# A retention layer and a bilinear FFN on one core: the output product of the last three tiles by Strassen's seven products

## The chip, the cores and the metric

The kernel runs on one core of a Trainium2 chip. The metric is the device time of one execution in microseconds (us). The kernel before took 224.37 us, the median of three runs (224.01 to 226.11).

The engines that appear below: TensorE (PE, with its weight loads as PEld) does the matmuls into PSUM, VectorE (DVE), ScalarE (ACT) and GpSimd (POOL) do everything elementwise, and SyncE (SP) issues the DMAs.

## The reference

Inputs are q, k and v of shape (4, 8, 768, 64), that is batch, heads, sequence and head size, and three weight matrices. For each batch and head a state of 64 x 64 decays by a factor gamma per step, and the tokens' results go through a bilinear FFN:

```python
for t in range(S):
    state = gamma[None, :, None, None] * state + np.einsum('bhd,bhe->bhde', k[:, :, t], v[:, :, t])
    y[:, :, t] = scale * np.einsum('bhd,bhde->bhe', q[:, :, t], state)
x = attn_out.transpose(0, 2, 1, 3).reshape(B * S, H * D)      # 3072 x 512
a = x @ w_a                                                   # 512 x 1536
b = x @ w_b                                                   # 512 x 1536
out = a * b @ w_out                                           # 1536 x 512, float32
```

## The kernel before, in words

The 3072 tokens are 24 **slots** of 128. `TILES = [4, 2, 2, 2, 2, 4, 4, 4]` groups the slots into eight FFN tiles J, of 512 or 256 tokens. The FFN's hidden size of 1536 is twelve chunks ft of 128.

**The FFN.** One *block* (J, ft) is `ffn_ab`: four matmuls `a` (L536, over the four chunks kt of the model size), a ScalarE copy of `a` to `asb` (L540), four matmuls `g` (L548), and a VectorE product `ht = g * asb` (L551), in bf16. After twelve blocks come the *outputs* (J, "o", i): for each slot i, `ffn_out` runs twelve matmuls of 512 columns with `ht` as the stationary operand and `wo_bf` as the moving one (L576), ScalarE copies the bank to `osb` (L180, called from L578), and SyncE stores it (L563 or L586). All of it is bf16 with float32 sums in PSUM. The banks `a`, `g`, `o` and one of the state banks come from one pool of three, `psff`.

**The retention.** Tokens are worked two slots at a time. `casts(t)` on GpSimd scales k and q of a slot by tables of the decay, to `kqb` (L210), and casts v (L182). A DMA transpose makes `kqT` (L223), and after the second slot of a pair the loads of the next pair are issued on SyncE (`load_slot`, L89), in the same queue as the transposes and the stores. A *turn*, `turn(new, old)`, is the TensorE work for two slots. It first runs the casts and leaves that are left in the list `later` (`catch_up`). For the older slots it does the first half of `inter` (q times the state, L320), for the newer ones `chunk_states` (k times v, L255, summed by VectorE into `sums`, L269, and cast to `gst`) and `scores` (k times q, L279, masked by VectorE into `aT`, L285), and for the older ones the second half of `inter` and `intra` (v times the masked scores, L332). Between the halves the rows of a PSUM bank change hands, so a *fence* is kept: a copy of one column, `mark`, on ScalarE or VectorE (L297), waits for the last matmul ahead of it, and the second half of `inter` waits for that copy. At the end `leave` copies the result to the FFN's input `xt` (L343, L349, L350).

**What sets the order.** Each engine runs its instructions in the order in which the code issues them (`seq`). The table `ahead` (L689 to L701) names what is issued ahead of each block or output: `(5, "o", 0): [(turn, 18, 16)]` is a turn ahead of tile 5's first output. Casts and leaves in `later` are issued by `catch_up`, two after each block, all of them ahead of an output.

## Time and profile before

| | |
|---|---|
| Time, median of three runs | 224.37 us (224.01 to 226.11) |
| Span of the profiled execution | 222.2 us (it has no time of its own beside the span) |
| Granted TensorE clock | full speed in all slices of the span |
| TensorE busy | 214.4 us |
| VectorE, ScalarE, GpSimd busy | 96.8, 93.7, 79.5 us |
| Matmuls of the outputs, L576 | 62.5 us busy in 299 matmuls |
| Matmuls `a` and `g`, L536 and L548 | 77.2 and 77.5 us busy, 401 each |
| GpSimd waiting for k (DMA) | 31.5 us |

Busy time of TensorE counts overlapping matmuls once. A row of a group reads: line, engine, operation, output and inputs, partitions by elements and type, count; then busy time in all and mean nanoseconds of one; then the idle time of that engine just ahead of them and what ended it. A row of the timeline reads: start, duration, engine, line, operation, count.

### The profile page before, as it was taken

The page shows a single profiled execution, that of the slowest core. Times are in us where ns is not written, and L with a number is a line of the kernel's source. Part 1 is how long each engine was busy: PE and PEld are TensorE (multiplying, and loading weights), DVE is VectorE, ACT ScalarE, POOL GpSimd, SP SyncE. Part 2 cuts the span into 40 slices and gives each one's busy share as a digit, 9 for nine tenths or more (in the row PEclk, how much of TensorE's full clock was granted, in tenths as well). Part 3 has the DMA queues.
Part 4 walks back from the last instruction along what each step waited for, and adds up shares of the span by engine and source line. Part 5 has one row for each costly group of instructions (what it writes and reads, how often), then busy time and mean ns, then how long its engine had stood idle before and what let it go on. Part 6 is the DMA issues. An engine that isn't in the chain of part 4 may idle for free.

```text
span 222.2 us, 6261 instructions
## 1 busy us (share of the span) xinstructions
PE 214.4 (96%) x2613; PEld 131.3 (59%) x2633; DVE 96.8 (44%) x199; ACT 93.7 (42%) x201; POOL 79.5 (36%) x105
## 2 busy tenths in 40 slices
PE   7799999999999999999999999999999999999994
PEld 6578655785457867867865444554444544444443
DVE  2783437641525535472475344533333621334300
ACT  3775244441535435443456333455333444333221
POOL 5557799682544335351613535350000000000000
PEclk9999999999999999999999999999999999999999
DMA  6999999999999988999969898984100012100022
GB/s 180 347 378 382 366 312 398 299 210 200 228 236 266 242 197 129 227 211 204 219 145 228 115 248 220 216 181 131 47 0 0 3 50 94 47 3 0 3 94 94
DMA packets 96124, 39.72 MB, mean 179 GB/s; under 512 B 76000, under 2 KB 91616, under 8 KB 96096
## 3 DMA queue, kind: packets, MB, share of 16 engines
q1 hardware_dynamic: 95952, 39.20, 68.5%
q8 instruction: 20, 0.33, 0.6%
q10 hardware_dynamic: 144, 0.13, 0.2%
q14 instruction: 8, 0.07, 0.1%
HBM read 28.31 MB, written 6.29 MB: 156 GB/s over the span
## 4 chain that ended last, share of the span: by engine, by line
PE 92%; DMA 3%; POOL 1%; issue 1%; DVE 1%; SPq 0%; ACT 0%; ACTq 0%; POOLq 0%
PE g L548 28%; PE a L536 28%; PE o L576 28%; DMA kf<-in_k_dram 3%; PE y L320 1%; POOL kqb L210 1%; PE at L279 1%; PE y L332 1%; PE st L255 1%; PE tp L395 1%; PE st L436 1%; DVE aT L420 1%; SPq L95 0%; PE at L408 0%; PE y L459 0%
## 5 line engine op out<-in xcount | busy, mean ns | idle before, releaser
L551 DVE TENSOR_TENSOR ht<-g,asb 128x256 bf16<-128x256 f32 (+1 forms) x98 | 53.9, 550 | 82.6 <-PE g L548 73.4
L548 PE MATMUL g<-xt,wb_bf 128*128 128x256 bf16 (+1 forms) x401 | 77.5, 317 | 0.2
L536 PE MATMUL a<-xt,wa_bf 128*128 128x256 bf16 (+1 forms) x401 | 77.2, 317 | 0.1
L540 ACT CAST asb<-a 128x256 bf16<-128x256 f32 (+1 forms) x98 | 46.3, 472 | 71.3 <-PE a L536 69.3
L576 PE MATMUL o<-wo_bf,ht 128*128 128x512 bf16 (+2 forms) x299 | 62.5, 362 | 1.4 <-issue 1.1
L536 PEld LDWEIGHTS <-wa_bf 128*128 128x128 bf16 x404 | 39.2, 98 | 23.5 <-DVE xt L182 0.4
L548 PEld LDWEIGHTS <-wb_bf 128*128 128x128 bf16 x404 | 39.4, 98 | 22.5
L576 PEld LDWEIGHTS <-ht 128*128 128x128 bf16 x312 | 28.8, 98 | 30.6
L210 POOL TENSOR_TENSOR kqb<-kf,ktab 128x512 bf16<-128x512 f32 x21 | 22.3, 1065 | 39.9 <-DMA kf<-in_k_dram 31.5
L180 ACT COPY osb<-o 128x512 f32<-128x512 f32 (+2 forms) x25 | 14.1, 564 | 36.1 <-PE o L576 27.8
L182 POOL CAST vb<-vf 128x512 bf16<-128x512 f32 x24 | 14.4, 610 | 23.0 <-DMA vf<-in_v_dram 18.5
L210 POOL TENSOR_TENSOR kqb<-qf,qtab 128x512 bf16<-128x512 f32 x21 | 22.3, 1063 | 0.1
L269 DVE TENSOR_TENSOR sums<-st,sums 128x256 f32<-128x256 f32 x30 | 12.7, 424 | 1.6
L180 ACT CAST gst<-sums 128x256 bf16<-128x256 f32 x26 | 10.4, 406 | 5.1 <-DVE sums L269 2.4
L285 DVE TENSOR_TENSOR aT<-at,mask 128x512 bf16<-128x512 f32 x18 | 11.5, 681 | 0.0
L343 ACT CAST xt<-y 128x512 bf16<-128x512 f32 x16 | 8.5, 584 | 0.7 <-PE y L332 0.7
L182 POOL CAST wo_bf<-wsto 128x1024 bf16<-128x1024 f32 x6 | 6.2, 1040 | 2.5 <-DMA wsto<-in_moe_w_out_dram 2.5
L182 POOL CAST wa_bf<-wsta 128x1024 bf16<-128x1024 f32 (+1 forms) x7 | 6.4, 919 | 1.7 <-DMA wsta<-in_moe_w_a_dram 1.6
L182 POOL CAST wb_bf<-wstb 128x1024 bf16<-128x1024 f32 (+1 forms) x7 | 6.4, 918 | 1.5 <-DMA wstb<-in_moe_w_b_dram 1.3
L395 PE MATMUL tp<-ident,kqb 128*128 128x128 bf16 x48 | 4.5, 220 | 1.6 <-DVE kqb L210 0.9
L320 PEld LDWEIGHTS <-gst 64*64 64x64 bf16 x264 | 3.7, 106 | 3.4 <-issue 3.4
L297 DVE COPY lgr<-bq 128x1 f32<-128x1 f32 x4 | 0.6, 154 | 11.2 <-PE y L320 11.2
(63 smaller groups left out, 99.2 us busy)
## 6 DMA issues: line engine op xcount, KB each, us to landing
out_dram<-osb SPq DMA_DIRECT2D x23, 256.0 KB, 2.7
kf<-in_k_dram SPq DMA_DIRECT2D x18, 256.0 KB, 4.2
qf<-in_q_dram SPq DMA_DIRECT2D x18, 256.0 KB, 4.4
vf<-in_v_dram SPq DMA_DIRECT2D x18, 256.0 KB, 4.9
wsta<-in_moe_w_a_dram SPq DMA_DIRECT2D x6, 512.0 KB, 7.6
wstb<-in_moe_w_b_dram SPq DMA_DIRECT2D x6, 512.0 KB, 7.8
wsto<-in_moe_w_out_dram SPq DMA_DIRECT2D x6, 512.0 KB, 8.5
kf<-in_k_dram SPq DMA_DIRECT2D x3, 512.0 KB, 5.9
```

What stands on the lines that cost most here:

```text
L180: seq(nc.scalar.copy(dst, src))
L182: seq(engine.tensor_copy(dst, src))
L210: seq(eng.tensor_tensor(dst, src, tab, op=ALU.mult))
L269: seq(nc.vector.tensor_tensor(new, u[c][:, s], old, op=ALU.add))
L285: seq(nc.vector.tensor_tensor(aT[n][:, r].rearrange("p s h d -> p (s h) d"), at[:, r].rearrange("p s h d -> p (s h) d"), mask.to_broadcast ...
L343: seq(nc.scalar.copy(dst, ys[o][c]))
L395: seq(nc.tensor.transpose(tp[:, m, hp, :], kqb[2 * u + par][:, i, hp, :, :], ident))
L536: seq(nc.tensor.matmul(a[:, b0 - c0 : b1 - c0], wa_bf[:, kt, fs], xcols(J, kt, b0, b1), start=(kt == 0 and b0 == c0), stop=(kt == KT - 1 a ...
L540: seq(nc.scalar.copy(asb, a))
L548: seq(nc.tensor.matmul(g[:, b0 - c0 : b1 - c0], wb_bf[:, kt, fs], xcols(J, kt, b0, b1), start=(kt == 0 and b0 == c0), stop=(kt == KT - 1 a ...
L551: seq(nc.vector.tensor_tensor(ht[J][:, ft, c0:c1], g, asbs.pop((J, ft, c0)), op=ALU.mult))
L576: seq(nc.tensor.matmul(o, ht[J][:, ft, i * P : (i + 1) * P], wo_bf[:, ft, c0:c1], start=(ft == 0), stop=(ft == NFT - 1)))
```

## The change

**The output product.** For tiles J >= `FAST` = 5, `ffn_out` per slot gives way to `ffn_fast` per pair of slots. The h of two slots (rows of even and odd tokens), the two chunks of a hidden pair (r = 0, 1) and the two halves of the 512 output columns form 2 x 2 blocks, and Strassen's algorithm in Winograd's form makes the four output blocks with seven products in place of eight. Each product is six matmuls of 256 columns. Four of the seven take sums of h (`hsum`, four per tile), which VectorE forms in bf16 block by block (`add`, by the table `adds`). Four take sums and differences of the weights (`wt_bf`): four VectorE operations and a ScalarE copy for each of six chunks, `combine_o`, after the outputs of tile 0 and the first of tile 1. Two banks are added to several times, R1 four times and R5 twice; between the additions ScalarE copies the bank to `snap`, or VectorE adds it to a copy.

**Layout.** In all tiles the columns of a pair of slots now stand even tokens first. To that end q of the later slots is loaded in two DMAs of 64 partitions instead of one of 128, the mask of the scores and the tables for q follow the new order (with another table on GpSimd), `queries` picks the columns of `kqT`, and a pair of slots is stored with one DMA of 512 KB instead of two of 256 KB. The late tables' VectorE and ScalarE part moves from the start into block 6 of tile 0.

**Order.** The turn (18, 16) moves from tile 5's first output to its block 8, the turn (22, 20) from tile 6's first output to its block 6, and the turn (None, 22) from tile 6's third output to its first. The marks of turns are always on ScalarE (before, four were on VectorE), casts to `gst` too, and leaves always come ahead of those casts. The masking of scores is put off by a block or output (`mask_now`). In the last leaves (turn without new slots) VectorE does both halves.

```diff
+FAST = 5
...
+            if nm == "q":
+                s = s.rearrange("h (n par) d -> par n h d", par=2)
+                for par in range(2):
+                    seq(nc.sync.dma_start(out=raws[nm, t][64 * par : 64 * par + 64], in_=s[par]))
+            else:
+                seq(nc.sync.dma_start(out=raws[nm, t], in_=s.rearrange("h p d -> p h d")))
...
+    def combine_o(j):
+        st = wst["o", j].rearrange("p r (c d) -> p r c d", c=2)
+        b11, b12, b21, b22 = st[:, 0, 0], st[:, 0, 1], st[:, 1, 0], st[:, 1, 1]
+        tmp = tra.tile([P, 2, DH], F32, tag="aT", name="tmp")
+        seq(nc.vector.tensor_tensor(tmp[:, 0], b12, b11, op=ALU.subtract))
+        seq(nc.vector.tensor_tensor(tmp[:, 1], b22, tmp[:, 0], op=ALU.subtract))
+        seq(nc.vector.tensor_tensor(wt_bf[:, j, 2], b22, b12, op=ALU.subtract))
+        seq(nc.vector.tensor_tensor(wt_bf[:, j, 3], b21, tmp[:, 1], op=ALU.subtract))
+        seq(nc.scalar.copy(wt_bf[:, j, :2], tmp))
...
             for s in range(2):
-                seq(nc.vector.tensor_tensor(dst[:, s, on], ys[o][c][:, s, on], part[:, s], op=ALU.add))
-                seq(nc.scalar.copy(dst[:, s, off], ys[o][c][:, s, off]))
+                seq(nc.vector.tensor_tensor(dst[:, s, on], src[:, s, on], part[:, s], op=ALU.add))
+                seq(nc.vector.tensor_copy(dst[:, s, off], src[:, s, off]))
...
             if new is not None:
-                fence[old, 0] = fence[old, 1] = fenced(eng)
+                fence[old, 0] = fence[old, 1] = fenced(nc.scalar)
...
+    def add(J, which, f0, f1):
...
+        x, y, op = {
+            0: (lambda: rows(J, 0, 1, f0, f1), lambda: rows(J, 1, 1, f0, f1), ALU.add),
+            1: (lambda: s[0], lambda: rows(J, 0, 0, f0, f1), ALU.subtract),
+            2: (lambda: rows(J, 0, 0, f0, f1), lambda: rows(J, 0, 1, f0, f1), ALU.subtract),
+            3: (lambda: rows(J, 1, 0, f0, f1), lambda: s[1], ALU.subtract),
+        }[which]
+        seq(nc.vector.tensor_tensor(s[which], x(), y(), op=op))
+
+    def product(R, J, u, left, right, first):
+        for f in range(NH):
+            if left[0] == "h":
+                r, par = left[1:]
+                lhs = ht[J][:, 2 * f + r, (2 * u + par) * P : (2 * u + par + 1) * P]
+            else:
+                lhs = hsum[J][left[1]][:, f, u]
+            w, m = right
+            seq(nc.tensor.matmul(R[:, :DH], lhs, (wo_bf, wt_bf)[w][:, f, m, :],
+                                 start=(first and f == 0), stop=(f == NH - 1), skip_group_check=True))
+
+    def ffn_fast(J, u):
+        osb, dst = placed[J, u] = place(J, u)
...
+        R1 = bank()
+        product(R1, J, u, ("h", 0, 0), (0, 0), True)
+        seq(nc.scalar.copy(snap[:, 0], R1[:, :DH]))
+        catch_up(2)
+        R6 = bank()
+        product(R6, J, u, ("h", 1, 0), (0, 2), True)
+        seq(nc.vector.tensor_tensor(osb[:, 0, :DH], R6[:, :DH], snap[:, 0], op=ALU.add))
+        mask_now(1)
+        catch_up(1)
+        store()
+        product(R1, J, u, ("s", 1), (1, 1), False)
+        seq(nc.scalar.copy(snap[:, 1], R1[:, :DH]))
+        catch_up(1)
+        R5 = bank()
+        product(R5, J, u, ("s", 0), (1, 0), True)
+        seq(nc.scalar.copy(snap[:, 2], R5[:, :DH]))
+        catch_up(1)
+        product(R1, J, u, ("s", 2), (1, 2), False)
+        seq(nc.vector.tensor_tensor(osb[:, 1, DH:], R1[:, :DH], snap[:, 2], op=ALU.add))
+        mask_now(1)
...
+        product(R5, J, u, ("s", 3), (0, 3), False)
+        seq(nc.vector.tensor_tensor(osb[:, 0, DH:], R5[:, :DH], snap[:, 1], op=ALU.add))
+        mask_now()
+        if ends:
+            seq(nc.sync.dma_start(out=dst[:, 0], in_=osb[:, 0]))
+        catch_up(1)
+        product(R1, J, u, ("h", 1, 1), (1, 3), False)
+        seq(nc.scalar.copy(osb[:, 1, :DH], R1[:, :DH]))
...
-        (1, "o", 1): [(turn, 8, 6, D_, True), (casts, 10)],
+        (1, "o", 1): [(turn, 8, 6), (casts, 10)],
...
-        (5, 2): [(casts, 21)], (5, "o", 0): [(turn, 18, 16)], (5, "o", 1): [(casts, 22)],
-        (5, "o", 2): [(turn, 20, 18, D_)], (5, "o", 3): [(casts, 23)],
-        (6, "o", 0): [(turn, 22, 20)], (6, "o", 2): [(turn, None, 22)],
+        (5, 2): [(casts, 21)], (5, 8): [(turn, 18, 16), (casts, 22)],
+        (5, "o", 2): [(turn, 20, 18), (casts, 23)],
+        (6, 6): [(turn, 22, 20)], (6, "o", 0): [(turn, None, 22)],
     }
...
+    adds = {3: [(0, 0, 2)], 4: [(1, 0, 2)], 5: [(2, 0, 2)], 6: [(3, 0, 2)],
+            7: [(0, 2, 4)], 8: [(1, 2, 4)], 9: [(2, 2, 4)], 10: [(3, 2, 4), (0, 4, 5)],
+            11: [(1, 4, 5), (0, 5, 6), (1, 5, 6), (2, 4, 5), (2, 5, 6), (3, 4, 5), (3, 5, 6)]}
...
+    combined = {(0, 0): (0, 1), (0, 1): (2,), (0, 2): (3,), (0, 3): (4,), (1, 0): (5,)}
```

What stands in a row on an engine, at three places. The first is ScalarE around the turn (8, 6), between tile 1's two outputs, before (the numbers of `gst` are those of its eight buffers):

```order
L180 COPY osb<-o 128x512 x3
L343 CAST xt<-y 128x2x4x64 x2
L180 CAST gst_157<-sums 128x256
L180 CAST gst_158<-sums 128x256
L180 COPY osb<-o 128x512
```

and after:

```order
L634 COPY osb<-o 128x512
L221 CAST wt_bf<-tmp 128x512
L337 COPY mark<-bq 128x1
L387 CAST xt<-y 128x2x8x32 x2
L199 CAST gst_157<-sums 128x256
L199 CAST gst_158<-sums 128x256
L199 CAST gst_159<-sums 128x256
L199 CAST gst_160<-sums 128x256
L634 COPY osb<-o 128x512
```

A copy of weight differences and the mark have come between the copy of the output and the leaves, and two casts that VectorE did. Second, ScalarE in tile 5's outputs, from the leaves of the turn (18, 16) on, before:

```order
L343 CAST xt<-y 128x2x4x64 x2
L180 COPY osb<-o 128x512 x2
L180 CAST gst_157<-sums 128x256
L180 CAST gst_158<-sums 128x256
L180 CAST gst_159<-sums 128x256
L180 CAST gst_160<-sums 128x256
L343 CAST xt<-y 128x2x4x64 x2
L180 COPY osb<-o 128x512 x2
```

and after, from the last copy of tile 5's first pair of slots to the last of its second, with the turn (20, 18) between them:

```order
L704 COPY osb<-o 128x256
L337 COPY mark<-bq 128x1
L677 COPY snap<-o 128x256
L387 CAST xt<-y 128x2x8x32 x2
L199 CAST gst_157<-sums 128x256
L686 COPY snap<-o 128x256
L199 CAST gst_158<-sums 128x256
L690 COPY snap<-o 128x256
L199 CAST gst_159<-sums 128x256
L199 CAST gst_160<-sums 128x256
L704 COPY osb<-o 128x256
```

The leaves and one cast now stand between the first and the second copy of a bank that TensorE goes on adding to. Third, VectorE at the end of tile 6's blocks, before (with the turns (22, 20) and (None, 22) behind):

```order
L551 TENSOR_TENSOR ht<-g,asb 128x512 x12
L269 TENSOR_TENSOR sums<-st,sums 128x256 x3
L285 TENSOR_TENSOR aT<-at,mask 128x512 x2
L349 TENSOR_TENSOR xt<-y,part 128x2x64 x4
L551 TENSOR_TENSOR ht<-g,asb 128x512 x12
```

and after, the last `ht` of tile 6 and the seven sums of h behind it:

```order
L597 TENSOR_TENSOR ht<-g,asb 128x512
L654 TENSOR_TENSOR hsum<-hsum,ht 128x256
L654 TENSOR_TENSOR hsum<-ht 128x256
L654 TENSOR_TENSOR hsum<-hsum,ht 128x256
L654 TENSOR_TENSOR hsum<-ht 128x256 x2
L654 TENSOR_TENSOR hsum<-ht,hsum 128x256 x2
```

The rows right behind these are the leaves of the turn (None, 22) and the three sums of the first pair of slots (L681, L693, L698):

```order
L394 TENSOR_TENSOR xt<-y,part 128x4x32
L395 CAST xt<-y 128x4x32
L394 TENSOR_TENSOR xt<-y,part 128x4x32
L395 CAST xt<-y 128x4x32
L394 TENSOR_TENSOR xt<-y,part 128x4x32
L395 CAST xt<-y 128x4x32
L394 TENSOR_TENSOR xt<-y,part 128x4x32
L395 CAST xt<-y 128x4x32
L681 TENSOR_TENSOR osb<-o,snap 128x256
L693 TENSOR_TENSOR osb<-o,snap 128x256
L698 TENSOR_TENSOR osb<-o,snap 128x256
```

The sums of the turn (22, 20) have gone into the blocks ahead, and seven sums of h and the eight operations of the last leaves stand between the last `ht` and the pair's first sum.

More of the change, by code (lines that the diff above doesn't have):

```diff
@@ L269, in chunk_states, with mask_now @@
                     seq(nc.vector.tensor_tensor(new, u[c][:, s], old, op=ALU.add))
-                eng = nc.vector if s and n in (8, 10, 12, 14) else nc.scalar
-                later.append(lambda i=2 * t + c + 1, new=new, eng=eng: cast(eng, gst[i % 8], new))
+                later.append(lambda i=2 * t + c + 1, new=new: cast(nc.scalar, gst[i % 8], new))
+    unmasked = []
+    def mask_now(n=100):
+        for fn in unmasked[:n]:
+            fn()
+        del unmasked[:n]
     def scores(n):
@@ L564, in store, with place @@
         held.clear()
+    def place(J, u):
+        n0 = (sum(TILES[:J]) + 2 * u) * P
+        osb = wstage.tile([P, 2, DM], F32, tag="w" + "ab"[u % 2], name="osb")
+        return osb, out[n0 : n0 + 2 * P, :].rearrange("(p two) d -> p two d", two=2)
+    placed = {}
     def ffn_out(J, i):
@@ L568, in ffn_out @@
         catch_up()
[L569 to L586 removed]
+        u, par = divmod(i, 2)
@@ new lines, in ffn_out @@
+        if par == 0:
+            placed[J, u] = place(J, u)
+        osb, dst = placed[J, u]
+        o = psff.tile([P, DM], F32, tag="ff", name="o")
+        for ft in range(NFT):
+            f, r = divmod(ft, 2)
+            seq(nc.tensor.matmul(o, ht[J][:, ft, i * P : (i + 1) * P],
+                                 wo_bf[:, f, 2 * r : 2 * r + 2, :].rearrange("p a d -> p (a d)"),
+                                 start=(ft == 0), stop=(ft == NFT - 1)))
+        seq(nc.scalar.copy(osb[:, par], o))
@@ new lines, in ffn_out, with rows @@
+        if par:
+            held.append((dst, osb))
+    hsum = {}
+    def rows(J, r, par, f0, f1):
+        h = ht[J].rearrange("p (f r) (u par m) -> p r f u par m", r=2, par=2, m=P)
+        return h[:, r, f0:f1, : TILES[J] // 2, par]
+    def add(J, which, f0, f1):
+        if J not in hsum:
+            hsum[J] = [wstage.tile([P, NH, 2, P], BF16, tag="w" + "ab"[i % 2], name="hsum") for i in range(4)]
+        s = [x[:, f0:f1, : TILES[J] // 2] for x in hsum[J]]
+        x, y, op = {
[5 more added lines that the diff above has]
+        seq(nc.vector.tensor_tensor(s[which], x(), y(), op=op))
@@ L654 @@
     for ft in range(2, NFT):
+        if ft == 6:
+            tables(*[argument(x) for x in late])
         if ft % FPW == 0 and ft // FPW + 1 < NW - 1:
@@ L704, in run, with visit, blocks @@
+    adds = {3: [(0, 0, 2)], 4: [(1, 0, 2)], 5: [(2, 0, 2)], 6: [(3, 0, 2)],
+            7: [(0, 2, 4)], 8: [(1, 2, 4)], 9: [(2, 2, 4)], 10: [(3, 2, 4), (0, 4, 5)],
+            11: [(1, 4, 5), (0, 5, 6), (1, 5, 6), (2, 4, 5), (2, 5, 6), (3, 4, 5), (3, 5, 6)]}
+    def visit(*at):
         for fn, *what in ahead.pop(at, []):
             fn(*what)
-        if len(at) == 2:
-            ffn_ab(*at)
-        else:
-            ffn_out(at[0], at[2])
-    for ft in range(NFT):
-        run(1, ft)
+    def blocks(J):
+        for ft in range(NFT):
+            visit(J, ft)
+            ffn_ab(J, ft)
+            if J >= FAST:
+                for which, f0, f1 in adds.get(ft, ()):
+                    add(J, which, f0, f1)
```

157 lines of the change are left out of this document (87 added, 70 removed).

## The prediction

> **What bounds the kernel now.** I read the page first: the busy shares, then the chain that ended last.
>
> ```profile
> span 222.2 us, 6261 instructions
> PE 214.4 (96%) x2613; PEld 131.3 (59%) x2633; DVE 96.8 (44%) x199; ACT 93.7 (42%) x201; POOL 79.5 (36%) x105
> PE 92%; DMA 3%; POOL 1%; issue 1%; DVE 1%; SPq 0%; ACT 0%; ACTq 0%; POOLq 0%
> ```
>
> TensorE is busy for 96% of the span and holds 92% of the chain. So a microsecond of matmuls removed is a microsecond gained, but only as long as nobody makes TensorE wait; the other engines are busy less than half of the time. What a matmul costs is not its duration, since they overlap, but the distance from one group's start to the next. Here is the timeline, first in the blocks of the last tile (512 columns), then in tile 1 (256 columns):
>
> ```profile
> 196.44 1.03 PE L536 MATMUL a<-xt,wa_bf 128*128 128x512 bf16 x4
> 197.31 1.03 PE L548 MATMUL g<-xt,wb_bf 128*128 128x512 bf16 x4
> ...
> 42.31 0.60 PE L548 MATMUL g<-xt,wb_bf 128*128 128x256 bf16 x4
> 42.64 0.42 PEld L536 LDWEIGHTS <-wa_bf 128*128 128x128 bf16 x4
> 42.74 0.60 PE L536 MATMUL a<-xt,wa_bf 128*128 128x256 bf16 x4
> 43.01 0.42 DVE L551 TENSOR_TENSOR ht<-g,asb 128x256 bf16<-128x256 f32 x1 [0.45 <-PE g L548]
> ...
> 43.38 0.37 ACT L540 CAST asb<-a 128x256 bf16<-128x256 f32 x1 [0.50 <-PE a L536]
> ```
>
> Four 512-column matmuls take .865, so .216 each; from 42.31 to 42.74 four of 256 columns take .435, and over longer stretches .109 each. The four weight loads between take .42, just below the .435, so a new weight per 256-column matmul is already paid in that pace. A group's shown end lies about .16 after its successor's start (42.31 + .60 = 42.91 against 42.74). From that shown end VectorE starts .10 later (43.01) and ScalarE .04 later (42.74 + .60 = 43.34, start 43.38).
>
> **The gain.** Before, each of the last twelve slots takes 12 matmuls of 512 columns: 144 x .2156 = 31.05 us, and about .1 more for the finer cut of the last slot. After, six pairs take 7 products of 6 matmuls of 256 columns: 252 x .1091 = 27.49. The difference is **-3.68**. One product lasts .654, one pair 4.58.
>
> **What the other engines then have to do.** These are the durations, by groups of the same shape:
>
> ```profile
> L551 DVE TENSOR_TENSOR ht<-g,asb 128x512 bf16<-128x512 f32 x46 | 31.8, 692 | 55.1 <-PE g L548 55.1
> L551 DVE TENSOR_TENSOR ht<-g,asb 128x256 bf16<-128x256 f32 x52 | 22.1, 425 | 27.5 <-PE g L548 18.3 <-ACT asb L540 9.2
> L182 DVE COPY qT<-tp 128x512 bf16<-128x512 bf16 x2 | 0.8, 424 | 0.8 <-PE tp L395 0.8
> L182 DVE CAST gst<-sums 128x256 bf16<-128x256 f32 x7 | 1.8, 290 | 0.0
> L349 DVE TENSOR_TENSOR xt<-y,part 128x128 bf16<-128x128 f32 x4 | 1.2, 292 | 5.4 <-ACT part L347 4.8 <-ACT xt L350 0.7
> L180 ACT COPY osb<-o 128x256 f32<-128x256 f32 x1 | 0.4, 373 | 0.7 <-PE o L576 0.7
> L180 ACT CAST vb<-vf 128x512 bf16<-128x512 f32 x1 | 0.6, 622 | 0.0
> L297 ACT COPY lgr<-bq 128x1 f32<-128x1 f32 x6 | 1.1, 192 | 2.8 <-PE y L320 1.8 <-PE y L459 1.0
> L180 ACT CAST gst<-sums 128x256 bf16<-128x256 f32 x26 | 10.4, 406 | 5.1 <-DVE sums L269 2.4 <-DVE sums L267 1.5
> L180 ACT CAST xt<-y 128x512 bf16<-128x512 f32 x4 | 3.0, 741 | 1.0 <-PE y L459 1.0
> ...
> 192.00:205.80 13.80, 13.70 (x64) 6.26 (x65) 5.52 (x9) 4.68 (x8) 0.00 (x0) 1.00 0.00 1
> ```
>
> The sums of h are the unknown: no operation in this trace adds two 16-bit operands of SBUF. Bounds from rows: the same operation with 32-bit input, .425 for 256 elements and .692 for 512; and the one operation with 16 bits on both sides, .424 for 512. The two .424 and .425 say that 512 elements of 16 bits cost what 256 of 32 bits do; taking off the part that does not grow (.425 - .267 = .158) leaves .158 + .134 = .29 for 256. I take **.42 and .29**, by the row that is nearest in type, and keep .69 and .425 for the range. [...]
>
> In the blocks the sums are free: by the window row VectorE is busy 5.52 in eight blocks of 1.725, .69 each, with 1.03 idle, and one add of .42 (at most .42 + .29) goes in. The six sets of weight differences (four VectorE operations of .42 and one ScalarE copy of .62 each) fall in the outputs of tiles 0 and 1, where VectorE waits for the next turn anyway; the late tables are four operations of at most .32 and are hidden as well. The cover that is missing is counted below.
>
> **Inside a pair** (start T). R1's first copy ends at T + .654 + .20 + .37 = 1.22, and TensorE, .06 later, may add to R1 again: 1.28, wanted at 1.31. The second and third copies come as narrowly, .02 to .03 ahead. None of the three waits should cost; a lag .05 longer makes six pairs .2 to .9 slower. I take **+.2**. The seventh product is different: it adds to R1 after VectorE has read it. The fifth ends at T + 3.27, VectorE starts at 3.53, ends at 3.95, TensorE goes on at 4.01 and could have at 3.92: .1, in the four pairs with nothing else, **+.4**.
>
> **First pair of each tile.** The last block's ht comes .26 + .69 = .95 after T. Behind it stand seven adds, which follow one another faster than their duration where they don't depend on each other:
>
> ```profile
> 116.63 0.49 DVE L182 CAST gst<-sums 128x256 bf16<-128x256 f32 x2
> ...
> 65.88 1.07 ACT L343 CAST xt<-y 128x512 bf16<-128x512 f32 x2 [0.70 <-PE y L332]
> 181.95 0.32 PE L320 MATMUL apart<-kqT,gst 64*64 64x64 bf16 x16
> 182.85 0.81 PE L576 MATMUL o<-wo_bf,ht 128*128 128x512 bf16 x3 [0.16 <-issue]
> ```
>
> Two casts of .29 in .49 make .20 from one to the next. The third add, on which the last matmul of the third product depends, ends by T + 1.64 to 1.82; that matmul starts at 1.31 + 5 x .109 = 1.85. No wait in tiles 5 and 7. In tile 6 the pair follows turn(None, 22), which lasts .8 to .9 in the trace (181.95 to 182.85), so T is .8 later, but VectorE now gets the eight operations of its leaving tile (.25 each, between .20 and .29) before R6's sum: .95 + 1.6 + 2.0 = 4.55, then two sums of .42 less overlap, 5.39 with the hand-over, against .78 + 3.92 = 4.70 for the seventh product: **+.7**.
>
> **Second pair of tile 5.** ScalarE copies R1 (to T + 1.23), then takes two leaves (1.07 by the row above, to 2.29) and a cast of .41 less overlap (2.65), before the copy which the fifth product waits for: 3.02, TensorE 3.08 against 2.62, **+.46**, with the seventh product's wait behind it **+.54**.
>
> **The fences.** Turns at an output had their mark on VectorE; now it stands behind ScalarE's copies. The first turn, before:
>
> ```profile
> 64.45 0.28 PE L320 MATMUL y<-kqT,gst 64*64 64x64 bf16 x10
> 64.60 0.59 ACT L180 COPY osb<-o 128x512 f32<-128x512 f32 x1 [2.00 <-PE o L576]
> 64.82 0.15 DVE L297 COPY lgr<-bq 128x1 f32<-128x1 f32 x1 [5.36 <-PE y L320]
> 65.17 0.29 PE L320 MATMUL y<-kqT,gst 64*64 64x64 bf16 x11
> ```
>
> The mark was over at 64.97 and TensorE came to it at 65.17, .72 after the turn's start: no wait. After, the osb copy ends at .74, the copy of weight differences .62 later, the mark .19 after that, TensorE .06: 1.61 against .72, **+.9**. Behind the waiting matmuls stand the turn's own leaves only. Turns (10, 8) and (16, 14) have no such weight copy: .99 against .72, about +.28 each. The turn in tile 5's outputs stands behind a copy of .37 and waits for nothing. Together **+1.45**. The turns that go into blocks find ScalarE idle: 0, and their masks and sums lie in VectorE's 1.03.
>
> **Start and end.** Four ScalarE leaves of the first tile lose their interleaved writes, .741 to about .54 (half of the 1.07 which two leaves of the later tiles take), one on the path: **-.15**. At the end:
>
> ```profile
> 219.15 0.27 ACT L180 COPY osb<-o 128x128 f32<-128x128 f32 x1 [0.97 <-PE o L576]
> 219.44 0.33 SPq L586 DMA_DIRECT2D out_dram<-osb  x1
> ...
> out_dram<-osb SPq DMA_DIRECT2D x23, 256.0 KB, 2.7
> out_dram<-osb SPq DMA_DIRECT2D x1, 128.0 KB, 1.7
> ```
>
> The last copy becomes .37 instead of .27, and a store of 256 KB is issued about .7 before TensorE's end, landing 2.7 later, instead of 128 KB and 1.7: **+.4**.
>
> **Sum:** -3.68 + .2 + .4 + .7 + .54 + 1.45 - .15 + .4 = **-.15**. The span would be 222.05. Between the profiled span (222.2) and the median of the runs (224.37) lie 2.2 us, which I keep: **224.2 us**.
>
> **Rivals.**
> 1. *The waits don't bite.* If fences, the ScalarE queue and the leaves of tile 6 are released earlier than I add up, 1.45 + .54 + .7 go: 224.2 - 2.7 = **221.5**. For it: in the old trace an engine's work overlaps more than durations say. Against: the two copies ahead of the first mark are in ScalarE's order and cannot be passed.
> 2. *The loads come late (slower).* Each load of q is now two DMAs of half the partitions, so a pair of slots has eight issues instead of six on SyncE, with the transposes behind them in the same queue.
>
> ```profile
> 99.48 0.57 SPq L89 DMA_DIRECT2D kf<-in_k_dram  x1
> ...
> 111.32 1.23 SPq L223 DMA_TRANSPOSE kqT<-kqb  x1
> ...
> 116.96 0.32 PE L320 MATMUL y<-kqT,gst 64*64 64x64 bf16 x16
> ...
> POOL kqb L210 <- DMA kf<-in_k_dram: 31.5, 8, 5.9
> DMA to landing us min/median/max: 2.7/3.5/5.3
> ```
>
> GpSimd waits 31.5 us for k, so the chain load, cast, transpose, next load sets the pace of the tiles. Two more issues of .57 + .05 cost 1.2 per pair if SyncE's issuing limits, nothing if the bytes do. The transpose of slot 17, issued at 111.32, lands by the median of 3.5 at 114.8; turn (16, 14), which needs it, starts at 116.96, so 2.2 us are spare. Four pairs of slots loaded before it make 4.8: it decides from a slip of 2.2 on, and gives up to +2.6: **226.8**. Against it: the later of the six issues take 1 to 2 us, which is waiting for transfers, and the time for two more is likely in there.
> 3. *The adds run at the 32-bit rate.* .135 longer each: seven in tile 6, +.95, and three ahead of the third product in tiles 5 and 7, 1.82 + .40 = 2.22 against 1.85, +.35 each: **225.8**.
> 4. *The change doesn't do what it says*: the 252 matmuls run no faster than the 144, because their weights (h, new for each) come slower than .109. That gives 224.2 + 3.6 = **227.8**. The weight loads of .42 per four in tile 1 speak against it.
>
> **Chances.** Forecast .58, rival 1 .13, rival 2 .15, rival 3 .11, rival 4 .03. The forecast's own range is 222.6 to 225.6 (fences 1.0 to 1.7, the copies 0 to .9, the pairs of tiles 5 and 6 by .35 each). With rivals 1 to 3 the range is **221.4 to 227.0**. One per cent, 2.2 us, is about what a measurement of this kernel tells from no change. Faster by more (below 222.1): rival 1 and a little of the forecast, .17. Slower by more (above 226.6): half of rival 2, rival 4, and rivals 2 and 3 falling on top of waits that are larger than mine, .21. Within: .62.
>
> **What would show it.** The three last tiles' output groups in the new profile should start .654 apart; six pairs of 4.58 plus waits. TensorE's idle time before matmuls should name VectorE at the seventh product of each pair, ScalarE at the fifth product of tile 5's second pair, and the ScalarE mark at the first turn, .9 there. VectorE's hsum group should show a mean near .42 and .29; .69 would be rival 3. TensorE waiting for the DMA of kqT at turn (16, 14) would be rival 2. I am wrong altogether if the outputs' pace is not .109 per matmul, or if waits appear in the tiles 0 to 4 where I have only the fences.

## The result and the profile after

The changed kernel took **225.70 us** (median of 20 runs, 224.96 to 228.39) beside 224.41 us for the kernel before (20 runs, 223.86 to 227.33). The ratio is **1.0052, 95% interval 1.0026 to 1.0077**: half a per cent slower, where the forecast was 0.1% faster. Medians are over all executions of a kernel; the ratios leave out those that are more than 1.5% above its fastest. Every execution here takes 1.7 us more than its span. The profiled one of the changed kernel, span 225.0, took 226.7, so it is 1.0 us above its median; the profiled one of before, span 222.2, took 223.9, 0.5 below its own. That is why the 2.8 us between the two spans are 1.3 between the medians.

The page of the changed kernel, with the lines that answer to those of before:

```profile
span 225.0 us, 6583 instructions
PE 214.5 (95%) x2717; PEld 140.6 (62%) x2717; DVE 128.7 (57%) x282; ACT 98.0 (44%) x225; POOL 81.8 (36%) x107
PE   8799999999999999997999999996999999999993
PE 79%; DMA 7%; issue 3%; DVE 3%; ACT 2%; POOL 2%; SPq 2%; DVEq 0%; ACTq 0%; POOLq 0%
```

TensorE still holds most of the chain (79%, before 92%), but "issue" went from 1% to 3%, and two slices out of forty (the 7 and the 6) are gaps in the middle. The waits of TensorE, by engine, line, what ended them, total, times and longest, tell which lines these belong to:

```profile
PE o L664 <- issue: 1.7, 1, 1.7
PE o L631 <- issue: 1.4, 1, 1.4
PE at L318 <- DMA kqT<-kqb: 0.2, 1, 0.2
PE g L594 <- ACT asb L586: 0.2, 1, 0.2
PE o L664 <- DVE hsum L654: 0.2, 1, 0.2
```

"Issue" means that nothing the profile shows was waited for. Before, the longest such wait on the outputs was 0.2 us. Here is TensorE's timeline at the two places, in tile 3's first output and in the second pair of slots of tile 5, eleven and eight matmuls after a turn:

```profile
98.72 2.55 PE L631 MATMUL o<-wo_bf,ht 128*128 128x512 bf16 x11
102.69 1.02 PE L631 MATMUL o<-wo_bf,ht 128*128 128x512 bf16 x4 [1.41 <-issue]
...
152.56 1.05 PE L664 MATMUL o<-wo_bf,ht 128*128 128x256 bf16 x8
155.30 0.60 PE L664 MATMUL o<-wo_bf,ht 128*128 128x256 bf16 x4 [1.69 <-issue]
```

The brackets count from the modelled end of the last matmul; from its start, less its own .216 or .109, TensorE lost 1.58 and 1.85 us. Both stops are in the middle of a group of matmuls, and the matmul at 155.30 has no semaphore to wait for at all.

Where the time went, read from the two timelines at the same points of the program:

| TensorE | before | after | behind by |
|---|---|---|---|
| first FFN matmul | 16.05 | 15.96 | -0.09 |
| turn (8, 6) starts | 64.45 | 64.92 | 0.47 |
| turn (8, 6) is over | 65.72 | 66.95 | 1.23 |
| turn (12, 10) starts | 95.90 | 97.30 | 1.40 |
| turn (14, 12) starts | 113.00 | 116.06 | 3.06 |
| turn (16, 14) starts | 116.96 | 120.02 | 3.06 |
| last matmul | 218.89 | 221.20 | 2.31 |
| end of the span | 222.2 | 225.0 | 2.8 |

The largest step, 1.66 between turns (12, 10) and (14, 12), is the first of the two waits. Behind turn (16, 14), where the seven products are, TensorE makes up less than 1 us, with the second wait in it. The products themselves run as forecast, here the last two pairs:

```profile
211.96 1.47 PE L664 MATMUL o<-wo_bf,ht 128*128 128x256 bf16 x12
213.27 2.13 PE L664 MATMUL o<-wt_bf,hsum 128*128 128x256 bf16 x18
215.23 0.82 PE L664 MATMUL o<-wo_bf,hsum 128*128 128x256 bf16 x6
215.98 0.81 PE L664 MATMUL o<-wt_bf,ht 128*128 128x256 bf16 x6
216.63 1.47 PE L664 MATMUL o<-wo_bf,ht 128*128 128x256 bf16 x12
```

A pair takes 216.63 - 211.96 = 4.67: seven times .654, and .09 before the seventh product.

A cause for the two waits could be read from the trace before any experiment, by counting. The trace records transfers of 16 KB on a queue of kind "instruction", 21 of them in the changed kernel (the row gives packets, MB and their share of the 16 DMA engines' time):

```profile
q8 instruction: 21, 0.34, 0.6%
```

TensorE's instructions (a weight load and a matmul each time) number 5,434, which makes 259 to a transfer. The two waits end at instructions 2746 and 4280 of TensorE, counted from the program's start: 1534 apart, six times 256 less two.

### The profile page after: what moved, and what is told of

Read it like the earlier page. It is cut to its first block, busy times and chain, and to the rows that moved or that the text cites. A ratio compares the mean times of both kernels' runs of the same rounds, so it can differ in the third digit from the quotient of the medians.

```text
span 225.0 us, 6583 instructions
## 1 busy us (share of the span) xinstructions
PE 214.5 (95%) x2717; PEld 140.6 (62%) x2717; DVE 128.7 (57%) x282; ACT 98.0 (44%) x225; POOL 81.8 (36%) x107
## 4 chain that ended last, share of the span: by engine, by line
PE 79%; DMA 7%; issue 3%; DVE 3%; ACT 2%; POOL 2%; SPq 2%; DVEq 0%; ACTq 0%; POOLq 0%
PE a L582 25%; PE g L594 25%; PE o L664 12%; PE o L631 10%; DMA qf<-in_q_dram 4%; DMA vf<-in_v_dram 2%; POOL kqb L240 2%; DMA kqT<-kqb 1%; PE y L360 1%; DVE ht L597 1%; PE y L372 1%; PE at L318 1%; DVE hsum L654 1%; PE tp L440 1%; PE y L519 1%
## 5 line engine op out<-in xcount | busy, mean ns | idle before, releaser
L631 PE MATMUL o<-wo_bf,ht 128*128 128x512 bf16 x144 | 32.6, 379 | 1.4 <-issue 1.4
L631 PEld LDWEIGHTS <-ht 128*128 128x128 bf16 x144 | 13.6, 98 | 17.0 <-issue 1.7
L201 POOL CAST vb<-vf 128x512 bf16<-128x512 f32 x24 | 15.3, 646 | 17.0 <-DMA vf<-in_v_dram 7.5
L664 PEld LDWEIGHTS <-hsum 128*128 128x128 bf16 x144 | 14.0, 98 | 2.1 <-DVE hsum L654 0.4
L634 ACT COPY osb<-o 128x512 f32<-128x512 f32 x12 | 7.0, 586 | 15.2 <-PE o L631 12.2
L664 PE MATMUL o<-wt_bf,hsum 128*128 128x256 bf16 x108 | 12.9, 273 | 0.2 <-DVE hsum L654 0.2
L664 PEld LDWEIGHTS <-ht 128*128 128x128 bf16 x108 | 10.4, 97 | 4.3 <-issue 1.9
L199 ACT CAST gst<-sums 128x256 bf16<-128x256 f32 x33 | 11.8, 412 | 0.1
L664 PE MATMUL o<-wo_bf,ht 128*128 128x256 bf16 x72 | 9.1, 273 | 1.7 <-issue 1.7
L654 DVE TENSOR_TENSOR hsum<-ht 128x512 bf16<-128x512 bf16 (+1 forms) x24 | 9.1, 391 | 0.2
```

Of the source, the lines that this page charges most:

```text
L199: seq(nc.scalar.copy(dst, src))
L201: seq(engine.tensor_copy(dst, src))
L631: seq(nc.tensor.matmul(o, ht[J][:, ft, i * P : (i + 1) * P], wo_bf[:, f, 2 * r : 2 * r + 2, :].rearrange("p a d -> p (a d)"), start=(ft == ...
L654: seq(nc.vector.tensor_tensor(s[which], x(), y(), op=op))
L664: seq(nc.tensor.matmul(R[:, :DH], lhs, (wo_bf, wt_bf)[w][:, f, m, :], start=(first and f == 0), stop=(f == NH - 1), skip_group_check=True))
```

## The experiments

The theory (A in the expectations) is that TensorE waited for its own program code, which by these counts arrives in pieces of about 256 instructions. The rivals are that something at these two places holds TensorE (B), the waits come with profiling (C), or they are real but small, and loads, fences and late tables make the kernel slow (D).

**Moving the code, not the work.** Ahead of the first data TensorE does warm-up matmuls. Cutting the same warm-up into more, narrower matmuls shifts all later instructions against the boundaries and changes nothing else.

```diff
-    warm(28, psat, "y1", 195, ones)
+    warm(42, psat, "y1", 130, ones)
```

> The changed kernel with 14 more, but narrower, warm-up matmuls at the start: 28 instructions more ahead of everything else. Theory A (code): the boundaries come 14 matmuls earlier, 3.0 us in the outputs of tile 3 and 1.5 us in the products of tile 5, in or near the turns, while the fetches begin at nearly the same time; the two waits move to the turns and grow, by up to 3.0 and 1.5 us, span 226 to 229 us. Theory B: both waits stay where they are, span 225 us. Theory C: timed ratio 1.005.

228.14 us, ratio 1.0167 (1.0120 to 1.0214): slower than the changed kernel by 1.1%. The timeline of this kernel's TensorE:

```profile
98.27 0.48 PE L372 MATMUL y<-aT,vb 64*64 64x64 bf16 x29
99.86 0.22 PE L372 MATMUL y<-aT,vb 64*64 64x64 bf16 x3 [1.12 <-issue]
...
124.05 0.82 PE L631 MATMUL o<-wo_bf,ht 128*128 128x512 bf16 x3 [0.78 <-issue]
...
152.88 0.52 PE L372 MATMUL y<-aT,vb 64*64 64x64 bf16 x25
155.10 0.25 PE L372 MATMUL y<-aT,vb 64*64 64x64 bf16 x6 [1.71 <-issue]
```

The waits left the outputs and now stand inside the turns, before other work, and a third has appeared. By count they are at the same instructions as before, 2746 and 4280, and the new one is at 3512, three times 256 ahead of the last. That rules out theory B. The waits did not grow as I had expected: they are 1.30 and 1.89 us, beside 1.58 and 1.85.

The same edit in the kernel before:

> The kernel before with 14 more, but narrower, warm-up matmuls at the start, 28 instructions, nothing else. Theory A: its boundaries move into the turns, where it had none by 0.1 us; waits of about 1.3 us at turn (12, 10) and up to 0.9 more at turns (16, 14) and (20, 18); span 223.5 to 225, ratio to the kernel before 1.005 to 1.012. Theory B (the waits come with the change: its 512 KB stores, its products): none appear, ratio 1.000.

227.00 us, ratio 1.0132 (1.0089 to 1.0175). Fourteen more, narrower warm-up matmuls alone make the kernel before 1.3% slower, more than the whole change does:

```profile
96.69 0.52 PE L332 MATMUL y<-aT,vb 64*64 64x64 bf16 x31
98.49 0.19 PE L332 MATMUL y<-aT,vb 64*64 64x64 bf16 x1 [1.28 <-issue]
...
123.51 0.38 PE L576 MATMUL o<-wo_bf,ht 128*128 128x512 bf16 x1 [1.39 <-issue]
```

These are two waits, at instructions 2750 and 3518, of 1.46 and 1.55; the second is larger than the 0.9 I had for turn (16, 14), and at turn (20, 18) there is none. It also rules out theory C: the two waits make 3.0 us in the profile, and the timed runs are 2.8 us slower.

The opposite shift, far:

```diff
-    warm(28, psat, "y1", 195, ones)
+    warm(21, psat, "y1", 256, ones)
...
-    warm(10, psat, "y1", 64)
+    warm(2, psat, "y1", 320)
...
-    warm(3, psat, "y1", 96)
+    warm(1, psat, "y1", 288)
...
-    warm(4, psat, "y1", 192)
+    warm(2, psat, "y1", 384)
```

> The changed kernel with 19 fewer, but wider, warm-up matmuls at the start, where TensorE waits for its first data: 38 instructions fewer ahead of everything else, the same work otherwise. Theory A (the two TensorE waits of 1.58 and 1.85 us in the changed kernel's profile, before instructions that wait for nothing, are waits for program code: they lie 1534 instructions apart, six times 256 less two, each behind a fetch of 16 KB): the code boundaries come 19 matmuls later, 4.1 us in the 512-column outputs and 2.1 us in the products, so both waits fall to at most 0.3 us; span 225.0 - 3 = about 222 us. Theory B (the waits belong to the place, a semaphore or a DMA of the data): both stay within 0.3 us, span 225 us. Theory C (they arise from profiling alone): the profile may do either, but the timed ratio to the kernel before stays at 1.005.

The two waits were gone from their places, as theory A says, but the time was 230.89 us (lowest 227.70, highest 233.71; ratio 1.0231), slower instead of 3 us faster. Two other waits had come, and in two stretches the granted clock was lower, so the time says nothing about the two waits that went. The clock row of its page:

```profile
PEclk9997999999997799999999999999999999999999
```

and its timeline:

```profile
16.25 0.36 PE L519 MATMUL y<-aT,vb 64*64 64x128 bf16 x11 [1.26 <-issue]
...
72.20 0.37 PE L360 MATMUL y<-kqT,gst 64*64 64x64 bf16 x10 [3.08 <-ACT mark L337]
```

The first is a code wait once more, at instruction 448 in the burst at the start. The second is the fence of turn (8, 6): its mark stands on ScalarE behind the weight difference, which here came late: VectorE's operations for this difference and the ones ahead of it took up to 1.26 us each beside GpSimd (last section). A lower clock follows each of these two waits in the page (the 7s of the row, in tenths of full speed); whether they caused it was not tried.

A smaller shift the same way, chosen so that no turn lies almost whole between two boundaries:

```diff
-    warm(10, psat, "y1", 64)
+    warm(2, psat, "y1", 320)
```

> The changed kernel with ten of its warm-up matmuls (64 columns) made two of 320 columns, at a place where TensorE waits for data in any case: 16 instructions fewer ahead of everything else, so the boundaries of 256 instructions come 8 matmuls later, 1.7 us in tile 3's outputs and 0.9 us in tile 5's, and the turn no longer lies whole between two of them with so little behind it. Theory A (code): the waits of 1.58 and 1.85 us fall to under 0.3 and under 1.0 us, none appears elsewhere; span 222.6 to 223, timed 1 to 2.5 us faster than the changed kernel, ratio to the kernel before 0.994 to 1.001. Theory C (the code waits are the profile's): ratio stays at 1.005. Rival D (loads, fences and late tables made the changed kernel slow in the timed runs): 1.005 as well.

224.10 us, ratio **0.9992** (0.9961 to 1.0022), against 1.0052 (1.0026 to 1.0077) of the changed kernel: 16 instructions fewer give 0.6% (give or take 0.4), which is the whole loss. So loads, fences and late tables, which are all still there, don't explain the loss by themselves (theory D). In the profile (span 222.6) the first wait is gone, the second is down to 0.72 at the same instruction 4280, and one of 0.54, which I had not expected, is at 3256. The row of the second in the timeline:

```profile
153.82 0.60 PE L664 MATMUL o<-wt_bf,hsum 128*128 128x256 bf16 x4 [0.56 <-issue]
```

And among this kernel's waits the fence of turn (8, 6), which now shows by itself (1.14 from start to start):

```profile
PE y L360 <- ACT mark L337: 1.0, 1, 1.0
```

Here are the larger code waits of these kernels, with the start of the last 16 KB transfer ahead of each. Instructions are counted as twice the weight loads, since some matmul records are missing from the traces:

```
kernel          instruction  mod 256   wait   ends at   transfer from   from there to the end
after                  2746      186   1.58    102.69           99.30                    3.39
after                  4280      184   1.85    155.30          152.56                    2.74
28 more (e2)           2746      186   1.30     99.86           97.41                    2.45
28 more (e2)           3512      184   0.94    124.05          121.68                    2.37
28 more (e2)           4280      184   1.89    155.10          152.41                    2.69
before, 28 more (e7)   2750      190   1.46     98.49           96.11                    2.38
before, 28 more (e7)   3518      190   1.55    123.51          120.54                    2.97
38 fewer (e1)           448      192   1.45     16.25           13.96                    2.29
16 fewer (e5)          3256      184   0.54    119.33          116.86                    2.47
16 fewer (e5)          4280      184   0.72    153.82          151.23                    2.59
```

The ten waits have this in common: each ended 2.3 to 3.4 us after its transfer began, and they stand at nearly the same remainder of 256, 184 to 192. In these ten cases the transfer in turn began 0.3 to 2.2 us after TensorE had entered the piece ahead (1.9 and 1.2 us in the changed kernel). A turn is 256 instructions in 1.2 to 1.4 us. In the changed kernel one lay nearly whole in each of the two pieces ahead of a wait, and TensorE was through with the turn and the few output matmuls behind it before it could go on with the next piece. In the kernel before, the piece with turn (12, 10) lasted from 95.99 to 99.62, and TensorE went on without a wait, 2.2 us after the transfer of the next had begun (97.42). That one transfer of 16 KB is one piece of 256 instructions is my reading of these remainders and of the 259 instructions to a transfer.

**Was the gain only luck that the kernel before was not given?** The same 16 instructions fewer in the kernel before:

> The kernel before with the same 16 instructions fewer at the start as in the two fast variants, so that what these gained is not owed to a placement of code that the kernel before was not given. Its turn (12, 10) lies between two boundaries with 3.3 us from one to the other, and a fetch took 2.3 to 3.4 us to serve: if some of its timed executions wait there, 0.1 to 0.5 us faster, ratio 0.998 to 1.000. If it never waits: 1.000.

224.46 us, ratio 1.0013 (0.9999 to 1.0027). There was nothing to gain there.

**Are the seven products worth their matmuls?** `FAST = 8`, so that all tiles use the eight products, with two stores moved accordingly:

```diff
-FAST = 5
+FAST = 8
```

> The changed kernel with FAST = 8: all tiles by eight products (12 matmuls of 512 columns per slot), no sums of h; the layout, the order, the fences, the weight differences (formed but not used) and the loads stay changed. If the seven products are worth what their matmuls say (3.7 us less their own waits of about 1.1 us in the profile), this is 2.6 us slower than the changed kernel apart from the code waits, some 228 us timed, ratio to the kernel before 1.015. If the products bring nothing, it is as fast as the changed kernel, 225.7, ratio 1.005. In the profile the startup and the turns should be late by the same 0.5 and 1.7 us as in the changed kernel.

226.84 us, ratio 1.0136 (1.0095 to 1.0177). Beside the run with 16 fewer instructions (0.9992), which has the products and like this one few code waits (0.29 here), the products are worth 1.4%, 3.2 us (give or take 1.1). In the two profiles, the stretch from the end of turn (16, 14) to the last matmul takes 100.29 us without them and 98.26 with them, 0.72 of code wait included; less that wait, the products save 2.75. The matmuls' 3.68 less the waits as measured, .54 (six of .09 before the seventh product) and .4 (first pair of tile 5), make 2.74. A part of the rest is the end: the whole last store of 512 KB is late here (span less last matmul 4.5 against 3.8). So everything else in the change costs about 3 us (the undivided last store in it), and the products about pay for it.

**Fences and late tables.** Three edits undone:

```diff
-        (1, "o", 1): [(turn, 8, 6), (casts, 10)],
+        (1, "o", 1): [(turn, 8, 6, D_), (casts, 10)],
...
-    combined = {(0, 0): (0, 1), (0, 1): (2,), (0, 2): (3,), (0, 3): (4,), (1, 0): (5,)}
+    combined = {(0, 0): (0, 1), (0, 1): (2,), (0, 2): (3,), (0, 3): (4,), (1, 1): (5,)}
...
     late = late_tables()
+    tables(*[argument(x) for x in late])
...
-        if ft == 6:
-            tables(*[argument(x) for x in late])
```

(and the marks of turns (10, 8) and (16, 14) likewise).

> The changed kernel with three of its edits undone: the late tables are formed at the start again, the marks of turns (8, 6), (10, 8) and (16, 14) are on VectorE again, and the last weight difference comes after tile 1's second output. If the late tables cost the 0.4 us wait in tile 0 (VectorE's 1.06 us multiplication beside GpSimd) and the marks 0.24, 0.24 and 0.16: 0.9 to 1.1 us faster than the changed kernel, 224.7 timed, ratio 1.000 to 1.001. If these waits only hide others (loads, casts): no change, 225.7, ratio 1.005. The wait of 0.41 us for the transposed slot at turn (8, 6) stays either way.

225.12 us, ratio 1.0042 (1.0016 to 1.0067), not to be told from the changed kernel's 1.0052, and not the 1.000 to 1.001 that I had expected. The profile does show the waits gone: turn (8, 6) starts at 63.98 instead of 64.92, and the marks hold nobody. But code waits of 0.69 and 1.69 stayed. With 16 instructions fewer on top:

> The run with marks on VectorE and the late tables at the start, and in addition the 16 instructions fewer at the start. Theory A: the waits of 0.69 and 1.69 us left in that run's profile fall to under 1.0 us together; span 220.5 to 221, timed 1 to 2.3 us faster than that run, ratio to the kernel before 0.990 to 0.997, the fastest so far. Theories C and D: 1.004 as that run had.

223.36 us, ratio **0.9960** (0.9936 to 0.9984), and the same kernel again on another chip:

> The kernel of the run with marks on VectorE, late tables at the start and 16 instructions fewer once more, beside the one above. If its 0.4 per cent over the kernel before is its own: ratio 0.994 to 0.998, and faster than the run above by the marks and late tables, 0.5 to 1 us less the 0.5 us that the leaves may give there. If it was that chip's: 0.998 to 1.002.

223.60 us, ratio 0.9979 (0.9955 to 1.0004). This version is the fastest, 0.2 to 0.4% ahead of the kernel before, but only one of its two intervals lies clear of 1. Its timeline still waits for the loads at turn (8, 6):

```profile
65.86 0.32 PE L319 MATMUL at<-kqT 64*64 64x64 bf16 x16 [0.55 <-DMA kqT<-kqb]
```

**The split loads alone**, in the kernel before:

```diff
+            if nm == "q":
+                for i in range(2):
+                    seq(nc.sync.dma_start(out=raws[nm, t][64 * i : 64 * i + 64],
+                                          in_=s[64 * i : 64 * i + 64]))
```

> The kernel before with each later load of q in two DMAs of 64 partitions, nothing else. If the eight loads per pair of slots delay the transposes as in the changed kernel (slot 9's issued at 62.80, there 1.1 us late beside the 0.5 us by which everything is), turn (8, 6) waits 0.4 to 0.7 us for it and turn (16, 14), with 2.2 us to spare, for nothing: ratio 1.001 to 1.003. If the chain falls behind by 1.2 us per pair: waits of up to 2.6 us at turn (16, 14), ratio 1.010. If SyncE has the time: 1.000.

224.84 us, ratio 1.0013 (0.9982 to 1.0043), no difference clear of the noise. The profile (span 223.4) names a price, though, at turn (16, 14), the place of rival 2: in its timeline the transpose of slot 17 is issued at 115.77 instead of 111.32, and the scores wait .87 (from start to start) for it.

```profile
115.77 1.24 SPq L229 DMA_TRANSPOSE kqT<-kqb  x1
...
118.54 0.32 PE L285 MATMUL at<-kqT 64*64 64x64 bf16 x16 [0.69 <-DMA kqT<-kqb]
```

**ScalarE's queue in tile 5's second pair.** In the kernels with fewer instructions this pair still waited 0.4 to 0.7. My step there was the leaves between the copies of R1, so they were put off:

```diff
-        catch_up(2)
+        free = (J, u) != (5, 1)
+        catch_up(2 if free else 0)
...
         seq(nc.scalar.copy(snap[:, 1], R1[:, :DH]))
-        catch_up(1)
+        catch_up(1 if free else 0)
```

> The fastest variant so far (marks on VectorE, late tables at the start, 16 instructions fewer), and in tile 5's second pair of slots the two leaves and a cast no longer stand on ScalarE between the first and the second copy of R1. If ScalarE's queue there is what TensorE waits for (0.43 us in that variant's profile, 0.72 in the other without code waits, nothing in the changed kernel, where a code wait of 1.85 us came just ahead of it): that wait falls below 0.15, 0.3 to 0.5 us faster than that variant, ratio to the kernel before 0.993 to 0.996. If something else is behind it (the sums of h, a bank): unchanged, 0.996.

223.92 us, ratio 0.9984 (0.9965 to 1.0003). Its profiled execution ran with the clock at 0.66 throughout (313 us), so the waits can't be read from it. The edit once more, on the kernel with the 16 instructions fewer alone:

> The changed kernel with 16 instructions fewer at the start, where the second pair of tile 5 waited 0.72 us without a code wait ahead of it, and with the two leaves and a cast of that pair taken from between the copies of R1. The last try of this edit gave a ratio of 0.998 and a profile from which nothing could be read. If ScalarE's queue is the cause: the wait falls below 0.15 in the profile, and the ratio is 0.996 to 0.998 where the same kernel without this edit had 0.999. If not: the 0.7 us stays.

224.18 us, ratio 1.0016 (0.9992 to 1.0040): no gain over the 0.9992 without the edit. And the wait is still there, with ScalarE idle ahead of its second copy, as the timeline of both engines shows:

```profile
151.65 0.59 ACT L387 CAST xt<-y 128x512 bf16<-128x512 f32 x1
...
153.07 1.36 PE L664 MATMUL o<-wt_bf,hsum 128*128 128x256 bf16 x11 [0.64 <-issue]
...
153.49 0.37 ACT L687 COPY snap<-o 128x256 f32<-128x256 f32 x1 [1.25 <-PE o L664]
```

It is the boundary at instruction 4280 again, so my step was wrong. What the ScalarE queue would cost without any code wait ahead of it was not seen in any run.

## Why the prediction was wrong

225.70 lies inside the range (221.4 to 227.0), but on the other side of no change than the forecast. It misses the forecast by 1.5 us, the profiled span misses its own (222.05) by 2.9: the profiled execution of before was half a microsecond faster than its median, the one after 1.0 slower. Step by step:

- **What bounds the kernel.** That "a microsecond of matmuls removed is a microsecond gained, but only as long as nobody makes TensorE wait" was right; the list of who can was short by one. The failed step is this one: I looked at engines, queues and DMAs, and never at the supply of instructions, which stands in the sum with nothing. It is also the largest error of the sum, 3.43 us in the profile (1.58 + 1.85). Less these, the profile would have ended about 0.65 before the old one, and the median moved from 225.7 to 224.1 when 16 instructions fewer took away 2.2 of the 3.4. My own sign of being wrong, a wait in the tiles 0 to 4 beside the fences, is the first of the two.
- **The change makes the second wait itself.** A product takes two instructions per .109, an output matmul of before two per .216. In the tile 5 pair the piece with turn (20, 18), from instruction 4024 on, would have been through in 2.1 us (151.35 to 153.45); before, the same stretch lasted from 148.37 to 155.09. The run with FAST = 8, whose boundaries lie elsewhere behind tile 5's first outputs, has no wait in tile 5's outputs. I counted the halved column width as gain only.
- **The gain**, -3.68, and .09 before the seventh product (forecast .1): right, and rival 4 is out with it. The other copies of R1 and R5: no waits, .2 too much.
- **The sums of h**: .42 and .29, as taken, wherever no GpSimd operation runs beside them, so rival 3 is out. These are two of their groups, then one of the weight differences and the first operation of the late tables:

```profile
L654 DVE TENSOR_TENSOR hsum<-ht 128x512 bf16<-128x512 bf16 x12 | 5.1, 426 | 0.2
L654 DVE TENSOR_TENSOR hsum<-ht,hsum 128x256 bf16<-128x256 bf16 x6 | 1.5, 286 | 0.0
L218 DVE TENSOR_TENSOR tmp<-wsto,tmp 128x256 f32<-128x256 f32 x6 | 3.9, 642 | 0.2
L152 DVE TENSOR_TENSOR earg<-posp1False,lgr 128x48 f32<-128x48 f32 x1 | 1.1, 1056 | 0.0
```

  At 512 elements such a sum of two bf16 inputs took .426, the product `ht` (float32, one input from PSUM) .692: less the .158 of my estimate for the part that doesn't grow, .27 against .53.
- **First pairs.** Tile 5 waited .41 where I had nothing, .34 of it because the first of the seven sums took .55 beside a GpSimd operation. Tile 6 waited .13 where I had .7, since the eight operations of the leaves followed one another by .20, as the casts in my own row did, not by .25.
- **Second pair of tile 5**, .54: not seen. In the changed kernel 1.85 of code wait came just ahead, in which ScalarE did its leaves.
- **Fences**, 1.45: turn (8, 6) lost .76 instead of .9, but only .16 of it to the mark; .23 went to the states and .41 to the transposed slot, both late for other reasons. In the run where the loads came in time the mark alone cost 1.14 (e5). Turns (10, 8) and (16, 14): .24 each, forecast .28.
- **Start**, -.15: the first FFN matmul came .09 earlier, but then the late tables, which I had called hidden in one sentence, cost about .56: from there to turn (8, 6) TensorE took 48.40 before, 48.96 after, and 48.41 in the run with the tables back at the start. VectorE's small multiplication took 1.06 us beside a GpSimd cast (27.30 to 28.34), against .21 in the run with the tables back at the start (e4: 208 ns), and ScalarE's `asb` and two banks waited behind it:

```profile
27.30 1.04 POOL L201 CAST wb_bf<-wstb 128x1024 bf16<-128x1024 f32 x1
27.34 1.06 DVE L152 TENSOR_TENSOR earg<-posp1False,lgr 128x48 f32<-128x48 f32 x1
29.42 0.81 PE L594 MATMUL g<-xt,wb_bf 128*128 128x512 bf16 x3 [0.20 <-ACT asb L586]
```

- **End**, +.4: 2.75 - 2.31 = .44, right.
- **The terms together.** What I had too small (start .6, tile 5's first pair .4) and too large (copies .2, tile 6 .6, tile 5's second pair .45, fences .2) nearly cancel. That the profile less its code waits comes near my sum is so far luck. (Redone from its printed numbers, the gain is -3.66 and the sum -.12; nothing hangs on that.)
- **Rival 2**, the loads: in the changed kernel turn (8, 6) waited .41 for a transpose, and turn (16, 14), where I put the price, nothing. With the loads split alone in the kernel before it was the other way round, .87 there and .24 at turn (8, 6). The mechanism exists; its timed price is not resolved.

What stays open: why the first of the two waits came in the changed kernel and not before, at the same instruction. The piece lasted as long (3.6 to 3.7 us without the wait), but its transfer began 1.9 us after the boundary instead of 1.4, and TensorE went on 3.4 us after that instead of 2.2. The transfer itself was no slower, 1.07 us beside 1.09; the difference lies between its end and TensorE's next instruction, 2.3 us beside 1.1, and the traces don't show what happens there.

## What to carry to other kernels

Where TensorE is busy for 96% of the span with small matmuls, count its instructions as well as its columns. In these runs its code came in transfers of 16 KB, 259 instructions to each by count, the waits stood 184 to 192 instructions past a multiple of 256, and TensorE went on 2.2 to 3.4 us after the transfer began, which was up to 2.2 us after the piece ahead was entered. The pieces that ended in a wait of the table held 1.3 to 4.0 us of work; others of 3.6 and 3.9 us passed without one. Cutting the columns per matmul in half took a matmul from .216 to .109 us, which by my estimate halves the time that a piece of such matmuls lasts. Where waits marked "issue" stand about a multiple of 256 instructions apart, as here (768, 1024 and 1534), move a few instructions ahead of them and time again, before a change is judged by half a per cent.

## What I had not expected of the hardware

- Fourteen more warm-up matmuls in idle time made the old kernel 1.3% slower (1.0089 to 1.0175), sixteen instructions fewer made the new one 0.6% faster.
- VectorE operations with two inputs in SBUF took longer in several places where they started while a GpSimd operation ran: 48 elements 1.06 us (27.34 to 28.40, beside a cast from 27.30 to 28.34) against .21 in the run with the late tables at the start (e4), weight differences of .42 up to 1.15 in the changed kernel (61.91 to 63.05, beside a GpSimd operation from 61.49 to 62.77) and 1.26 in the run with 38 instructions fewer. A sum of h that began .04 ahead of a GpSimd operation (145.30) took its usual .41.
